# Exchanging row maxima and row sums between partition groups: copies in place of one-element reduces, and a later place for the row-sum reciprocal

## The chip, the cores and the metric

The kernel runs on one core of a Trainium2 chip. The metric is the device time of one execution in microseconds. TensorE (PE), VectorE (DVE), ScalarE (ACT) and GpSimd (POOL) run side by side, each in its own program order, and wait for each other by semaphores.

## The reference, cut to what matters

```python
# attention: batch 8, heads 8, seq 576, head_dim 64, float32
scores = scale * q @ k.T
thresh = max(scores, -1) - tau
attn   = exp(where(scores >= thresh, scores, -1e9) - max(scores))
attn   = attn / (sum(attn, -1) + 1e-9)
x      = attn @ v                       # to 4608 x 512
# feed-forward, d_ff 1536
out    = (silu(x @ w_gate) * (x @ w_val)) @ w_out
```

## The kernel before

From the second batch on (28 of 32 head pairs, 140 score tiles) the kernel works on "halved" tiles. The 128 partitions are four groups of 32. Two neighbouring groups hold the same 32 query rows, one against the first half of the keys, the other against the second. A row's maximum and its sum are therefore in two partition groups, and each group must fetch the other's value. That is the function meet:

```python
def meet(x, m):                                  # x: [128, m, 2 or 3]; m = 4, or 2 for the last tile of a pair
    for g in range(NG):                          # four groups
        o = g ^ 1                                # the neighbour
        nc.vector.tensor_reduce(out=x[g*G:(g+1)*G, 0:m, 1], in_=x[o*G:(o+1)*G, 0:m, 0:1],
                                axis=AX.X, op=ALU.max)      # a reduce over one element: a copy

def scores(seg, t):                              # a generator; halved case, cut
    # TensorE: scores into the PSUM tiles pss (two, or one for the last tile of a pair); there are two in all
    for x, tile_ in enumerate(pss):
        nc.vector.tensor_reduce(out=mx[:, 2*x:2*x+2, 0], in_=tile_[:, :, 0:SH], ..., op=ALU.max, negate=True)
    meet(mx, m)
    nc.vector.tensor_reduce(out=nm[:, 0:m], in_=mx[:, 0:m, :], axis=AX.X, op=ALU.min)
    nc.scalar.activation(th[:, 0:m], nm[:, 0:m], AF.Identity, bias=cut, scale=-1.0)
    for x in range(m):
        nc.scalar.activation(ps[x], scs[x], AF.Exp, bias=nm[:, x:x+1])
    yield
    turn(1)                                      # VectorE transposes an earlier tile
    for x in range(m):                           # threshold and row sum; frees the score PSUM
        nc.vector.scalar_tensor_tensor(out=ps[x], in0=scs[x], scalar=th[:, x:x+1], in1=ps[x],
                                       op0=ALU.is_ge, op1=ALU.mult, accum_out=sm[:, x, 0:1])
    meet(sm, m)
    nc.vector.tensor_reduce(out=tot[:, 0:m], in_=sm[:, 0:m, :], axis=AX.X, op=ALU.add)
    nc.vector.reciprocal(out=ri[:, 0:m], in_=tot[:, 0:m])
    yield
    for x in range(m):                           # scaling, on GpSimd
        nc.gpsimd.tensor_scalar(out=ps[x], in0=ps[x], scalar1=ri[:, x:x+1], scalar2=None, op0=ALU.mult)
    yield

# main loop, per tile, cut: the feed-forward products of earlier batches fill TensorE's time
go = scores(seg, t); next(go)
next(go); fill(part); next(go); fill(part)
```

## Time and profile before

| | before |
|---|---|
| median of 6 runs | 1625.6 us (1624.4 to 1627.6) |
| TensorE busy | 95% of the span |
| VectorE busy | 67% |
| GpSimd busy | 48%; 480 us of it are the 486 scalings of L319 |
| both exchanges on VectorE | 1120 reduces of about 0.15 us |

The prediction below shows most of the lines.

### The profile page before, as it was taken

Reading aid. Unit: us, or ns where it says so; the run is one execution under the profiler, and the core shown is the slowest. Engines: PE = TensorE matmul, PEld = TensorE weight load, DVE = VectorE, ACT = ScalarE, POOL = GpSimd, SP = SyncE. Lnnn points to the kernel's source line nnn. Section 1 sums busy time; section 2 is a strip of 40 time slices with the busy share of each in tenths; the row PEclk is TensorE's granted clock in tenths of the full one; section 3 lists DMA queues with packets and bytes.
Section 4 is the critical chain, followed back from the end, with each engine's and each line's share of the span. In section 5 each row is a group of like instructions: output and inputs, shape, how many; then the busy total and the mean of one; then the engine's idle time right before and its main releaser. Section 6 shows DMA issues by size and latency. Waiting matters only on the chain.

```text
span 1625.3 us, 29972 instructions
## 1 busy us (share of the span) xinstructions
PE 1548.6 (95%) x11344; PEld 1033.4 (64%) x11344; DVE 1081.0 (67%) x3618; ACT 604.1 (37%) x1304; POOL 780.6 (48%) x726
## 2 busy tenths in 40 slices
PE   6898779889999999999999999999999999999998
PEld 4675555347675776657666766675755675677865
DVE  6887888787777777767767777776776787500000
ACT  6776644223333333333333333343434343311110
POOL 3554455555555555545555455554655554511111
PEclk9899889999999999999999999999999999999999
DMA  7541221111111111011111111101111110000000
GB/s 171 144 138 59 69 50 30 43 43 31 37 37 37 37 37 31 18 32 37 30 43 37 37 37 30 39 13 36 31 43 37 37 31 28 1 14 7 7 13 13
DMA packets 176415, 66.82 MB, mean 41 GB/s; under 512 B 159632, under 2 KB 159632, under 8 KB 176272
## 3 DMA queue, kind: packets, MB, share of 16 engines
q1 hardware_dynamic: 173328, 55.47, 15.1%
q0 software_dynamic: 2944, 9.44, 1.7%
q8 instruction: 90, 1.47, 0.4%
q14 instruction: 53, 0.43, 0.1%
HBM read 55.44 MB, written 9.44 MB: 40 GB/s over the span
## 4 chain that ended last, share of the span: by engine, by line
PE 78%; DVE 9%; POOL 1%; ACT 1%; issue 1%; POOLq 0%; DVEq 0%; ACTq 0%
PE po L488 21%; PE pg L442 21%; PE pv L442 20%; PE sc L267 8%; PE xa L400 8%; DVE p L307 2%; DVE mx L287 2%; DVE p L333 1%; POOL p L319 1%; DVE mx L244 1%; ACT p L303 1%; DVE sums L244 0%; DVE wo L185 0%; ACT L303 0%; POOL ht L473 0%
## 5 line engine op out<-in xcount | busy, mean ns | idle before, releaser
L319 POOL TENSOR_SCALAR p<-p,ri 128x288 f32<-128x288 f32 x486 | 480.3, 1004 | 504.4 <-DVE ri L315 504.3
L442 PE MATMUL pg<-xall,wgv 128*128 128x256 f32 (+1 forms) x1824 | 403.0, 374 | 5.7 <-POOL wgv L190 5.7
L442 PE MATMUL pv<-xall,wgv 128*128 128x256 f32 (+1 forms) x1824 | 399.9, 373 | 0.0
L442 PEld LDWEIGHTS pg<-xall,wgv 128*128 128x128 f32 x1824 | 331.4, 192 | 75.7 <-issue 19.2
L442 PEld LDWEIGHTS pv<-xall,wgv 128*128 128x128 f32 x1824 | 331.0, 191 | 60.4 <-issue 11.6
L488 PE MATMUL po<-wo,ht 128*128 128x512 f32 x816 | 364.2, 598 | 4.6 <-POOL ht L473 4.6
L307 DVE SCALAR_TENSOR_TENSOR p<-sc,th,p 128x288 f32<-128x288 f32 (+1 forms) x540 | 258.7, 529 | 57.2 <-ACT p L303 56.1
L488 PEld LDWEIGHTS po<-wo,ht 128*128 128x128 f32 x816 | 151.1, 190 | 196.1 <-issue 186.2
L299 ACT ACTIVATE th<-nm,cut 128x4 f32<-128x4 f32 (+1 forms) x140 | 41.6, 297 | 539.7 <-DVE nm L290 539.7
L303 ACT ACTIVATE p<-sc,nm 128x288 f32<-128x288 f32 (+1 forms) x540 | 237.2, 512 | 0.7
L287 DVE TENSOR_REDUCE mx<-sc 128x2 f32<-128x576 f32 x252 | 179.5, 749 | 77.7 <-PE sc L267 77.6
L267 PE MATMUL sc<-kT,qT 64*32 64x288 f32 x4032 | 170.9, 415 | 29.4 <-DVE p L307 29.3
L462 DVE TENSOR_TENSOR ht<-gt,pv 128x512 f32<-128x512 f32 (+1 forms) x108 | 69.8, 646 | 191.6 <-PE pv L442 186.3
L333 DVE STREAM_TRANSPOSE p<-p 128x576 f32<-128x576 f32 x252 | 181.4, 754 | 4.3 <-POOL p L319 4.3
L473 POOL TENSOR_TENSOR ht<-ht,gt 128x512 f32<-128x512 f32 (+1 forms) x108 | 127.9, 1211 | 80.1 <-ACT gt L471 80.1
L267 PEld LDWEIGHTS sc<-kT,qT 64*32 64x32 f32 x4032 | 66.5, 106 | 121.8 <-issue 96.6
L400 PE MATMUL xa<-p,vall 64*64 64x288 f32 x2016 | 131.8, 412 | 9.8 <-issue 7.4
L456 ACT COPY gt<-pg 128x512 f32<-128x512 f32 (+1 forms) x114 | 65.0, 570 | 156.6 <-PE pg L442 156.6
L400 PEld LDWEIGHTS xa<-p,vall 64*64 64x64 f32 x2016 | 80.4, 135 | 60.9 <-issue 16.8
L244 DVE TENSOR_REDUCE sums<-sums 32x4 f32<-32x4 f32 (+1 forms) x560 | 83.9, 150 | 10.5
L411 DVE COPY xall<-xa 128x128 f32<-128x128 f32 x56 | 13.7, 286 | 115.2 <-PE xa L400 115.2
L244 DVE TENSOR_REDUCE mx<-mx 32x4 f32<-32x4 f32 (+1 forms) x560 | 83.1, 148 | 10.4
(78 smaller groups left out, 969.5 us busy)
## 6 DMA issues: line engine op xcount, KB each, us to landing
vall<-in_v_dram SPq DMA_DIRECT2D x112, 144.0 KB, 3.2
qraw<-in_q_dram SPq DMA_DIRECT2D x128, 72.0 KB, 2.4
kraw<-in_k_dram SPq DMA_DIRECT2D x128, 72.0 KB, 2.7
out_dram<-ob POOLq DMA_DIRECT2D x32, 256.0 KB, 2.4
wo<-in_moe_w_gate_dram SPq DMA_DIRECT2D x16, 384.0 KB, 3.5
wo<-in_moe_w_val_dram SPq DMA_DIRECT2D x16, 384.0 KB, 4.0
xall<-in_moe_w_out_dram SPq DMA_DIRECT2D x6, 768.0 KB, 5.3
wo<-in_moe_w_out_dram SPq DMA_DIRECT2D x2, 768.0 KB, 4.3
```

The source lines that it names most:

```text
L244: nc.vector.tensor_reduce(out=x[g * G:(g + 1) * G, 0:m, 1], in_=x[o * G:(o + 1) * G, 0:m, 0:1], axis=AX.X, op=ALU.max)
L267: nc.tensor.matmul(ps[g * G:(g + 1) * G, u, 0:SH], qT[hs, col + a * G:col + (a + 1) * G], kT[hs, c * SH:(c + 1) * SH], start=True, stop=True)
L287: nc.vector.tensor_reduce(out=mx[:, 2 * x:2 * x + 2, 0], in_=tile_[:, :, 0:SH], axis=AX.X, op=ALU.max, negate=True)
L303: nc.scalar.activation(ps[x], scs[x], AF.Exp, bias=nm[:, x:x + 1])
L307: nc.vector.scalar_tensor_tensor(out=ps[x], in0=scs[x], scalar=th[:, x:x + 1], in1=ps[x], op0=ALU.is_ge, op1=ALU.mult, accum_out=sm[:, x, ...
L319: nc.gpsimd.tensor_scalar(out=ps[x], in0=ps[x], scalar1=ri[:, x:x + 1], scalar2=None, op0=ALU.mult)
L333: nc.vector.transpose(out=p, in_=p)
L400: nc.tensor.matmul(xa[a][h * D:(h + 1) * D, at:at + n * G].rearrange("d (i q) -> d i q", q=G), vr[rs, h, j, :], p[rs, lo:lo + n, j, :], st ...
L442: nc.tensor.matmul(ps[:, i], wgv[:, mat, c, (f + i) * P:(f + i + 1) * P], x[:, c, cs], start=(c == 0), stop=(c == NCC - 1))
L462: nc.vector.tensor_tensor(out=hts[f // 2][:, :, 0:n], in0=gts[f // per][:, f % per:f % per + GR, :], in1=ps, op=ALU.mult)
L473: nc.gpsimd.tensor_tensor(out=ht, in0=ht, in1=gt[:, 2 * x:2 * x + 2, :], op=ALU.mult)
L488: nc.tensor.matmul(po, hts[f // 2][:, f % 2, i * P:(i + 1) * P], wo[:, f, :], start=(f == 0), stop=(f == NF - 1))
```

## The change

The intent, as it reads: take the exchange of sums off VectorE, give it to ScalarE, and compute sum and reciprocal later in VectorE's order, so that ScalarE's answer has time to come. With it, meet takes the copying function as an argument, and the maxima are now exchanged by VectorE's tensor_copy in place of the one-element tensor_reduce.

```diff
-    def meet(x, m):
+    def meet(x, m, copy):
         for g in range(NG):
             o = g ^ 1
-            nc.vector.tensor_reduce(out=x[g * G:(g + 1) * G, 0:m, 1], in_=x[o * G:(o + 1) * G, 0:m, 0:1],
-                                    axis=AX.X, op=ALU.max)
+            copy(x[g * G:(g + 1) * G, 0:m, 1:2], x[o * G:(o + 1) * G, 0:m, 0:1])
...
-            meet(mx, m)
+            meet(mx, m, nc.vector.tensor_copy)
...
-            meet(sm, m)
+            meet(sm, m, nc.scalar.copy)
+            yield
             nc.vector.tensor_reduce(out=tot[:, 0:m], ...)
...
         nc.vector.reciprocal(out=ri[:, 0:m], in_=tot[:, 0:m])
-        yield
+        if not halved:
+            yield
```

## The prediction

> **What bounds the kernel now.** I read the page's busy table first, then the windows by stage, then who waited for whom, then the timeline of single tiles. From the page:
>
> ```profile
> PE 1548.6 (95%) x11344; PEld 1033.4 (64%) x11344; DVE 1081.0 (67%) x3618; ACT 604.1 (37%) x1304; POOL 780.6 (48%) x726
> L319 POOL TENSOR_SCALAR p<-p,ri 128x288 f32<-128x288 f32 x486 | 480.3, 1004 | 504.4 <-DVE ri L315 504.3
> L244 DVE TENSOR_REDUCE sums<-sums 32x4 f32<-32x4 f32 (+1 forms) x560 | 83.9, 150 | 10.5
> L244 DVE TENSOR_REDUCE mx<-mx 32x4 f32<-32x4 f32 (+1 forms) x560 | 83.1, 148 | 10.4
> ```
>
> TensorE is the busiest engine. The two L244 groups are the exchanges that the change touches: 140 halved score tiles x 4 partition groups, for the row maxima (mx) and the row sums (sums). By stage (before the halved tiles; their first part, with the weights still being put together; the long part; the tail with feed-forward work alone):
>
> ```profile
> 0.00:166.00 166.00, 139.62 (x962) 96.93 (x963) 126.81 (x267) 115.72 (x211) 76.14 (x49) 0.94 0.46 126
> 166.00:345.00 179.00, 145.90 (x1148) 86.42 (x1146) 151.16 (x508) 73.27 (x164) 99.32 (x85) 0.90 0.22 52
> 345.00:1405.00 1060.00, 1052.44 (x8409) 700.99 (x8401) 784.26 (x2806) 385.09 (x874) 569.83 (x559) 1.00 0.15 33
> 1405.00:1625.30 220.30, 210.66 (x838) 149.09 (x836) 18.74 (x39) 30.05 (x55) 35.29 (x35) 0.99 0.03 10
> ```
>
> The columns are the stretch, its length, busy us of PE, PEld, DVE, ACT, POOL, then clock and DMA. From 345 to 1405 us PE is idle for only 7.6 us of 1060: nothing taken off another engine can gain more than that there. From 166 to 345 it is idle for 33 us, with DVE 84% busy. What PE waits for:
>
> ```profile
> PE sc L267 <- DVE p L307: 29.3, 22, 4.5
> PE xa L400 <- issue: 7.4, 1, 7.4
> ```
>
> So the only loop around PE that the change touches is: scores (sc) on PE, maximum of scores on DVE (L287), exchange of maxima (L244), nm (L290), exp on ACT, threshold and row sum on DVE (L307), which frees the two score buffers in PSUM for the next scores. One tile of it, with PE's load rows left out:
>
> ```profile
> 769.12 1.20 PE L267 MATMUL sc<-kT,qT 64*32 64x288 f32 x32
> ...
> 769.78 0.18 DVE L315 RECIPROCAL ri<-tot 128x4 f32<-128x4 f32 x1
> ...
> 770.05 3.95 POOL L319 TENSOR_SCALAR p<-p,ri 128x288 f32<-128x288 f32 x4 [6.47 <-DVE ri L315]
> ...
> 770.45 1.42 DVE L287 TENSOR_REDUCE mx<-sc 128x2 f32<-128x576 f32 x2
> 771.90 0.64 DVE L244 TENSOR_REDUCE mx<-mx 32x4 f32<-32x4 f32 x4
> 772.57 0.16 DVE L290 TENSOR_REDUCE nm<-mx 128x4 f32<-128x8 f32 x1
> ```
>
> The reader is to see that the exchange of maxima (771.90) begins while GpSimd is in its four scalings of the previous tile (770.05 to 774.00), and now is not held up by them: four reduces in 0.64 us, the usual.
>
> **What the Trainium skill says.** "SBUF — State Buffer", § Who interferes with whom: VectorE and GpSimd share one pair of SBUF ports under an exclusive lock; a VectorE copy in a 2-port mode takes it and waits for a GpSimd instruction in progress, while tensor_reduce never does on this chip. "VectorE: DVE Perf Modes", § What auto-detection actually checks: a one-source copy with both ends in SBUF and an even outer dimension goes into the 2-port mode by itself. The new exchange of maxima is a tensor_copy of 32x4 or 32x2 float32 in SBUF, so it qualifies. The trace of before has the same conflict with other instructions, two-port tensor_scalars of the weight work:
>
> ```profile
> 224.47 1.80 POOL L190 TENSOR_TENSOR wo<-wo,spare 128x768 f32<-128x768 f32 x1
> ...
> 224.57 2.25 DVE L181 TENSOR_SCALAR wo<-wo 128x768 f32<-128x768 f32 x1
> ```
>
> That L181 form takes 0.66 us in the median. Begun 0.1 us after a GpSimd instruction it took 2.25, to 0.5 us after GpSimd ended. The lock is real here; what no run has yet is how it treats four tiny copies against a train of four GpSimd instructions. "VectorE: DVE Perf Modes", § The TRN2 errata: a small SBUF operation costs mostly a fixed time per instruction; the trace agrees (142 to 156 ns for 2 or 4 elements), so a copy is hardly cheaper than the reduce it replaces. Same page, § Two Vector instructions with no wait between them: an instruction whose operands start in another quadrant than those before starts only after these have finished. Each of the four copies changes quadrant, so I expect them one after the other with a gap in which GpSimd can take the lock back.
>
> **The change part by part.**
> (1) Exchange of sums moves to ACT. DVE loses 560 x 0.150 = 84 us, ACT gains 560 copies; ACT's smallest copy now, 64x32, takes 180 ns, so about 100 us: ACT goes from 604 to some 705 us, 43% of the span. ACT has no part in the lock. The copies sit in ACT's order after the exps and before the evacuation of the next gate product, and wait for the last L307; that holds an evacuation by up to 1 us, which the four product buffers in PSUM should cover: 0 on PE. For DVE the saving counts only where DVE is the limit: the seven or so tiles between 166 and 230 us with weight pieces on DVE, 7 x 0.64 = 4.5 us. Elsewhere the work lay beside PE's scores (in the tile above DVE is done with ht before mx begins): 0.
> (2) tot and reciprocal come after the first half of the fill. In the instruction order of the changed kernel, 95 of the 140 tiles have nothing between L307 and tot: there DVE waits for the ACT copies, about 0.1 + 4 x 0.18 = 0.8 us in place of 0.64 on its own, so ri is 0.1 to 0.2 us later. In 40 tiles a product with the value branch (0.66 us) comes first, and in 5 weight work. GpSimd's scalings so start 0.2 to 1 us later, nearer to the next exchange of maxima. Their consumer, DVE's transposition, comes over a tile later (scaled 801.1 to 805.1, transposed 815.5), so this alone costs nothing.
> (3) Exchange of maxima becomes 560 DVE copies: without the lock, 0 to 10 ns each, nothing. With the lock: I followed GpSimd's work through the timeline at each of the 139 exchanges that have a later score tile. 99 begin while GpSimd is busy; its unbroken work then lasts another 1.88 us in the mean (186 us in all), but the single instruction in progress only 0.61 us (60 us in all). If the four copies have to take turns with the four scalings, the exchange is stretched by the first number, else by the second.
> How much reaches PE I took from each next score tile's slack: how long L307 had been done when PE got to it. In 345 to 1405, 29 of 118 tiles have under 0.3 us of it, 40 have 0.3 to 1.7 (mostly 1.5, a tile with one gate and one value product), 49 more; in 166 to 345, 17 of 21 have none. Stretch minus 0.1 us minus slack, where positive, sums to 20.7 + 62.9 = 84 us if turns are taken, and 6.2 + 10.6 = 17 us if not. Moving the scalings of the tiles with a value product between makes the first 99 us and leaves the second as it is.
> Sum: 1625 - 4.5 + 1 (the later ri) + something from 17 to 99. I don't hold the turn-taking for sure on every copy (in one place of the trace a GpSimd tensor_scalar let a VectorE instruction in halfway), so I take about 40: 1662 us.
>
> **The rivals.**
> A, no conflict at all: the copies are so short that they slip in. Then only (1) and (2) count: 1615 to 1626. Against it: every L181 that began under a GpSimd instruction was longer than its median.
> B, one wait per exchange: once the first copy has the lock, the other three follow before GpSimd's next. GpSimd's scalings follow each other at 0.985 us with records of 1.004, so its next is always ready. 1630 to 1645.
> C, turns for every copy: 1690 to 1725.
> D, the ACT round trip hurts: DVE waits for ACT in 95 tiles, and ACT may be late where it has sigmoids, table loads (1.28 us) or weight pieces ahead. 1625 to 1640, with no long copies. For it: the idle time before tot would appear. Against it: DVE waits for PE's scores just after anyway, 77.7 us at L287.
> I give A 0.15, B and D together 0.30, something between B and C 0.35, C 0.20.
>
> **Range and chances.** Slower by over 2% begins at 1657.8 us: all of C and most of between, 0.20 + 0.30 = 0.50, and a little of the others, 0.52. Faster by over 2% needs 32 us of PE idle time given back, nearly all of that in 166 to 345: 0.02. The rest 0.46. The range that should hold it 8 times in 10 leaves out the best part of A and the worst of C: 1622 to 1708.
>
> **What would show it.** Right: L244 copies of mx with a mean well over 0.15 us and single ones near 1 us, all where a POOL L319 runs; PE sc waiting for DVE p L307 grown from 29.3 us by the added time; 345 to 1405 with PE idle time; ACT near 705 us; sums copies of about 0.18 us on ACT; tot with idle time before it that ACT ended. Wrong: mx copies of 0.14 us beside L319, then the lock does not matter for such small copies and the time stays at 1615 to 1626; or a longer time with short copies, then it is D or PE waiting for an evacuation on ACT.

## More of the kernel before

One more view, part 4 of the page, is the chain that ended last, followed back from the end of the program; its shares tell which engine the end hung on:

```profile
PE 78%; DVE 9%; POOL 1%; ACT 1%; issue 1%; POOLq 0%; DVEq 0%; ACTq 0%
```

The end hangs mostly on TensorE, so a change on another engine shows up only if it makes TensorE wait longer or shorter.

## The result, and the profile after

The changed kernel takes 1701.5 us (median of 6 runs, 1697.3 to 1706.2). The ratio to the kernel before is 1.0467, with a 95% interval of 1.0446 to 1.0488: 76 us slower. Ratios here are the mean time of one kernel's fast runs over that of the other's fast runs of the same rounds, so not quite the ratio of the medians quoted; "so many us" below means the ratio minus one, times the 1626 us of before.

From the page after (lines of the kernel are moved by one or so; L319 of before is L320, L307 is L306):

```profile
PE 1585.5 (93%) x11344; PEld 1048.8 (62%) x11344; DVE 1103.2 (65%) x3058; ACT 716.3 (42%) x1864; POOL 779.6 (46%) x726
...
PE 66%; DVE 17%; ACT 5%; issue 2%; POOL 2%; DMA 0%; SPq 0%; DVEq 0%; POOLq 0%; ACTq 0%
...
L244 DVE COPY mx<-mx 32x4 f32<-32x4 f32 (+1 forms) x560 | 189.8, 339 | 10.5
...
L244 ACT COPY sums<-sums 32x4 f32<-32x4 f32 (+1 forms) x560 | 108.5, 194 | 165.5 <-DVE p L306 158.7
...
L312 DVE TENSOR_REDUCE tot<-sums 128x4 f32<-128x12 f32 (+1 forms) x140 | 23.0, 164 | 97.0 <-ACT sums L244 97.0
```

Three things stand out. VectorE executes 560 instructions fewer and is still busy 22 us longer. The exchange of maxima went from 83.1 to 189.8 us, 339 ns a copy in place of 148. And tot, which had nothing to wait for, now has 97 us of idle time before it, ended by ScalarE's copies. The chain of the end hangs on VectorE for 17% in place of 9%. What TensorE waits for, after:

```profile
PE sc L266 <- DVE p L306: 68.8, 49, 5.2
PE po L489 <- POOL ht L474: 9.1, 3, 4.0
```

The wait of the scores for L306, which frees the score buffers, went from 29.3 us in 22 waits to 68.8 us in 49. This counts only waits that the profile shows as idle time. PE's busy time grew as well, by 37 us (1548.6 to 1585.5). Of these, 18.5 us lie on the score matmuls (170.9 to 189.4), where a wait in the middle of a group, and the slower clock told of next, may be counted as busy. The other half lies on matmuls that don't wait for VectorE's score work. It goes with a slower TensorE: the mean granted clock (1 is full speed) was 0.981 to 0.987 in the runs of before and 0.969 to 0.974 in all six of the changed kernel. In stretches at half clock a gate or value matmul took 634 ns, elsewhere 379 (medians of both traces). From 345 us on, TensorE was never busy at half clock in the profile of before, and for 36 us in this one. By an estimate from these figures (36 us times 1 - 379/634) that costs about 15 us. No run holds the clock apart, so whether the waits bring it down is not shown.

The single copies are uneven: 156 ns at the least, 172 in the middle, 1703 at the most:

```profile
L244 DVE COPY mx<-mx x560: 156/172/1703, 167.5 to 1480.4; 32x4 f32<-32x4 f32 x150, 32x2 f32<-32x2 f32 x37
```

Where they are long, GpSimd is at work: the longest of the 143 copies that meet no tensor instruction of GpSimd in this trace took 0.31 us. From the timeline of the changed kernel, VectorE and GpSimd in one stretch (start, duration, instruction):

```profile
828.44 1.42 DVE L286 TENSOR_REDUCE mx<-sc 128x2 f32<-128x576 f32 x2 [1.69 <-PE sc L266]
828.79 3.72 POOL L474 TENSOR_TENSOR ht<-ht,gt 128x512 f32<-128x512 f32 x3
829.24 0.56 ACT L457 COPY gt<-pg 128x512 f32<-128x512 f32 x1
829.89 3.36 DVE L244 COPY mx<-mx 32x4 f32<-32x4 f32 x4
```

Four copies of four elements took 3.36 us in place of 0.64. The first three ended with GpSimd's three products (at 830.08, 831.30 and 832.54; the products at 830.06, 831.28 and 832.51), and the fourth took 0.70 us beside the query scaling that followed. Looked at one by one in narrower stretches of the same time, one copy and the product it had to sit out are:

```profile
830.02 1.26 POOL L474 TENSOR_TENSOR ht<-ht,gt 128x512 f32<-128x512 f32 x1
830.10 1.21 DVE L244 COPY mx<-mx 32x4 f32<-32x4 f32 x1
```

The copy begins 0.08 us after the product, ends 0.02 us after it, and the next copy (831.32) sits out the next product in the same way. Beside the scalings it is milder:

```profile
814.33 1.00 POOL L320 TENSOR_SCALAR p<-p,ri 128x288 f32<-128x288 f32 x1
814.39 0.46 DVE L244 COPY mx<-mx 32x4 f32<-32x4 f32 x1
```

Here the copy was done at 814.85, halfway through the scaling, which itself took no longer than usual. No copy that met scalings of L320 alone took over 1.01 us; the 27 copies of over 1.1 us met products, query scalings or weight work.

### The profile page after: what moved, and what is told of

Its sections match the earlier page's. It is cut to its first block, busy times and chain, and to the rows that moved or that the text cites. A ratio compares the mean times of both kernels' runs of the same rounds, so it can differ in the third digit from the quotient of the medians.

```text
span 1702.9 us, 30134 instructions
## 1 busy us (share of the span) xinstructions
PE 1585.5 (93%) x11344; PEld 1048.8 (62%) x11344; DVE 1103.2 (65%) x3058; ACT 716.3 (42%) x1864; POOL 779.6 (46%) x726
## 4 chain that ended last, share of the span: by engine, by line
PE 66%; DVE 17%; ACT 5%; issue 2%; POOL 2%; DMA 0%; SPq 0%; DVEq 0%; POOLq 0%; ACTq 0%
PE pg L443 17%; PE po L489 17%; PE pv L443 17%; PE sc L266 8%; PE xa L401 7%; DVE mx L244 5%; DVE p L306 4%; DVE mx L286 3%; DVE p L334 2%; ACT L302 1%; ACT p L302 1%; POOL p L320 1%; ACT sums L244 1%; DVE nm L289 0%; DVE wo L185 0%
## 5 line engine op out<-in xcount | busy, mean ns | idle before, releaser
L320 POOL TENSOR_SCALAR p<-p,ri 128x288 f32<-128x288 f32 x486 | 479.2, 1001 | 545.5 <-DVE ri L315 483.1
L443 PE MATMUL pv<-xall,wgv 128*128 128x256 f32 (+1 forms) x1824 | 405.7, 376 | 0.0
L489 PE MATMUL po<-wo,ht 128*128 128x512 f32 x816 | 370.8, 607 | 9.1 <-POOL ht L474 9.1
L443 PEld LDWEIGHTS pv<-xall,wgv 128*128 128x128 f32 x1824 | 335.1, 194 | 63.1 <-issue 14.0
L306 DVE SCALAR_TENSOR_TENSOR p<-sc,th,p 128x288 f32<-128x288 f32 (+1 forms) x540 | 258.6, 530 | 57.5 <-ACT p L302 56.6
L266 PE MATMUL sc<-kT,qT 64*32 64x288 f32 x4032 | 189.4, 427 | 69.4 <-DVE p L306 68.8
L244 DVE COPY mx<-mx 32x4 f32<-32x4 f32 (+1 forms) x560 | 189.8, 339 | 10.5
L266 PEld LDWEIGHTS sc<-kT,qT 64*32 64x32 f32 x4032 | 71.7, 108 | 173.2 <-issue 144.8
L244 ACT COPY sums<-sums 32x4 f32<-32x4 f32 (+1 forms) x560 | 108.5, 194 | 165.5 <-DVE p L306 158.7
L312 DVE TENSOR_REDUCE tot<-sums 128x4 f32<-128x12 f32 (+1 forms) x140 | 23.0, 164 | 97.0 <-ACT sums L244 97.0
```

What stands on the lines that cost most here:

```text
L244: copy(x[g * G:(g + 1) * G, 0:m, 1:2], x[o * G:(o + 1) * G, 0:m, 0:1])
L266: nc.tensor.matmul(ps[g * G:(g + 1) * G, u, 0:SH], qT[hs, col + a * G:col + (a + 1) * G], kT[hs, c * SH:(c + 1) * SH], start=True, stop=True)
L443: nc.tensor.matmul(ps[:, i], wgv[:, mat, c, (f + i) * P:(f + i + 1) * P], x[:, c, cs], start=(c == 0), stop=(c == NCC - 1))
L489: nc.tensor.matmul(po, hts[f // 2][:, f % 2, i * P:(i + 1) * P], wo[:, f, :], start=(f == 0), stop=(f == NF - 1))
```

## The experiments

Two theories were open: the VectorE copies of the maxima held up by GpSimd ("the lock"), and the round trip over ScalarE with the later reciprocal. Twelve kernels ran; all gave right results.

### Taking the two parts of the change apart

**e1_max_reduce.** The changed kernel, with the maxima by reduce again:

```diff
-            meet(mx, m, nc.vector.tensor_copy)
+            meet(mx, m, reduce_copy)      # the one-element tensor_reduce
```

> The changed kernel, with the maxima exchanged by tensor_reduce again; sums on ScalarE and the later sum and reciprocal stay. If VectorE's copies of the maxima, held up by GpSimd, cost the time: 1616 to 1632 us, PE sc waiting for L306 about 25 to 35 us as before. If the ScalarE round trip and the later reciprocal cost a good part of it: 1650 to 1685 us, with the waits of tot for ACT (97 us in the changed kernel) still there. If the two only hurt together: near 1625 here and near 1625 in the next run too.

Measured: 1634.1 us, ratio 1.0044 (1.0027 to 1.0060): +7 us, 2 us above the range for held-up copies. TensorE's wait for L306's counterpart and tot's wait for ScalarE:

```profile
PE sc L269 <- DVE p L309: 32.9, 27, 3.7
...
DVE tot L315 <- ACT sums L244: 97.0, 130, 1.4
```

Most of the loss is gone, though ScalarE's copies and the wait for them are all there.

**e2_max_copy_only.** The kernel before, with only the maxima by copy:

```diff
-            meet(mx, m)                   # reduces
+            meet(mx, m, nc.vector.tensor_copy)
```

> The kernel before, with the maxima exchanged by VectorE copies and nothing else changed. Held-up copies as the cause: 1675 to 1705 us, copies of mx near 0.34 us in the mean as in the changed kernel. ScalarE round trip as the cause: 1625 to 1645 us. A part each: 1650 to 1675.

Measured: 1690.7 us, ratio 1.0394 (1.0378 to 1.0409): +64 us, nothing moved to ScalarE. Its exchange lines:

```profile
L244 DVE COPY mx<-mx 32x4 f32<-32x4 f32 x448 | 150.4, 336 | 8.4
L247 DVE TENSOR_REDUCE sums<-sums 32x4 f32<-32x4 f32 x448 | 67.3, 150 | 8.4
L244 DVE COPY mx<-mx 32x2 f32<-32x2 f32 x112 | 35.4, 316 | 2.1
```

The copies take 185.8 us against the 83.1 of the reduces. So one call in the diff, which the change's intent does not speak of, carries 64 of the 76 us. With e1's 7 that makes 71; the 5 left lie at the edge of the intervals.

**e3_early_sum.** The changed kernel, with tot and reciprocal right after ScalarE's copies:

```diff
             meet(sm, m, nc.scalar.copy)
-            yield
             nc.vector.tensor_reduce(out=tot[:, 0:m], ...)
```

> The changed kernel with tot and reciprocal emitted right after the exchange of sums, so that VectorE waits for ScalarE in all 140 tiles. If the late place matters by moving GpSimd's scalings into the exchange of maxima: faster than the changed kernel by 10 to 20 us, 1680 to 1692. If the place matters little: 1695 to 1710.

Measured: 1709.2 us, ratio 1.0506 (1.0490 to 1.0523). It is slower than the changed kernel, not faster, by about 6 us; the guess that the late place drives GpSimd into the exchange at a net cost fell. Given ScalarE's copies, the late place is the better one.

**e4_sum_copy_only.** The kernel before, with the sums by VectorE copies and the maxima by reduces:

```diff
-            meet(sm, m)                   # reduces
+            meet(sm, m, nc.vector.tensor_copy)
```

> The kernel before, with the sums exchanged by VectorE copies and the maxima by reduces. The same 560 copies as in the second run, at another place of the tile, where GpSimd's scalings of the tile before are mostly done. Lock theory: few copies held up, mean under 0.2 us, 1622 to 1640 us. If a copy between quadrants is slow in itself, wherever it stands: as much as the second run.

Measured: 1626.0 us, ratio 0.9999 (0.9984 to 1.0014). Its copies:

```profile
L244 DVE COPY sums<-sums 32x4 f32<-32x4 f32 x448 | 75.4, 168 | 8.5
```

The same 560 copies on the same engine cost nothing here: at this place of the tile the scalings are mostly over, and a copy takes 168 ns. In the trace 131 of the 140 exchanges of sums meet no GpSimd work; the few that do are held up here too, up to 1.36 us for one copy. So it is not the copy that is slow but the copy beside GpSimd.

### Is it the lock?

**f3_max_copy_to_psum.** The changed kernel whole, but the copies of the maxima write to unused columns of the score tile in PSUM:

```diff
-            meet(mx, m, nc.vector.tensor_copy)
-            nc.vector.tensor_reduce(out=nm[:, 0:m], in_=mx[:, 0:m, :], axis=AX.X, op=ALU.min)
+            other = pss[0][:, 0, SH + 32:SH + 32 + m]
+            for g in range(NG):
+                o = g ^ 1
+                nc.vector.tensor_copy(other[g * G:(g + 1) * G], mx[o * G:(o + 1) * G, 0:m, 0])
+            nc.vector.tensor_tensor(out=nm[:, 0:m], in0=mx[:, 0:m, 0], in1=other, op=ALU.min)
```

> The changed kernel whole, but the VectorE copies of the maxima write to unused columns of the score tile in PSUM, and the minimum of own and other maxima is a tensor_tensor. Same count of copies at the same place, with one end in PSUM, where the two-port mode needs both in SBUF. Lock theory: no copy over 0.3 us although GpSimd runs beside them, time 1630 to 1640 as with reduces. If a small copy between quadrants is slow beside any GpSimd work, or by its place in the tile: 1690 to 1705.

Measured: 1638.2 us (1634.5 to 1643.3), ratio 1.0072 (1.0047 to 1.0097); the interval overlaps that of e1. All its copies (shortest, middle, longest):

```profile
L291 DVE COPY sc<-mx x560: 150/162/169, 164.8 to 1410.0; 32x4 f32<-32x4 f32 x150, 32x2 f32<-32x2 f32 x37
```

Same operation, same count, same place, GpSimd as busy as ever (780 us; 118 of the 140 exchanges begin while it works): with one end outside SBUF the longest of 560 copies took 169 ns, against 1703. This is the behaviour that the lock of the two-port mode asks for, and a slow copy between partition groups does not.

**f4a_act_scaling** is a base: the kernel before, with the scalings on ScalarE in place of GpSimd (the diff shows this edit). **f4b_act_scaling_max_copy** is the same with the maxima by VectorE copies:

```diff
-            if halved and not split:      # scaling on GpSimd
+            if False:                     # always on ScalarE
```

> The kernel before with the 486 scalings of the probabilities on ScalarE in place of GpSimd, as a base for the next run; both exchanges by reduce. ScalarE gets about 280 us more and stays under 60% of the span: 1625 to 1660.

> The run before this one, with the maxima exchanged by VectorE copies. If GpSimd's work beside the copies is the cause, and the scalings the larger part of it: copies of mx under 0.25 us in the mean (0.336 with the scalings on GpSimd), and only 10 to 40 us above the run before this one, from the output products and the query scaling that stay on GpSimd. If GpSimd's scalings have little to do with it: 55 us or more above it.

Measured: f4a 1634.1 us, ratio 1.0053 (1.0038 to 1.0068); f4b 1672.2 us, ratio 1.0292 (1.0274 to 1.0309). The copies cost 38 us here (1.0292 / 1.0053, times 1626), where they cost 64 with the scalings on GpSimd.

```profile
L244 DVE COPY mx<-mx 32x4 f32<-32x4 f32 x448 | 105.1, 235 | 8.4
L244 DVE COPY mx<-mx 32x2 f32<-32x2 f32 x112 | 20.5, 183 | 2.1
```

In f4b's timeline, 117 of the 140 exchanges meet no GpSimd work and take 0.68 us in the mean. The other 23 meet output products, query scalings or weight work and are stretched by 37 us together. So a few long hold-ups cost almost what they last, and taking the scalings away removes 26 of the 64 us. I had expected the scalings to be the larger part; they are the more frequent one but not the costlier one.

### The rest: ScalarE's round trip and the late place

**f1_late_only** is the kernel before with only the late place of tot and reciprocal, both exchanges by reduce. **f2_act_sums_early** is the kernel before with only the sums on ScalarE, tot and reciprocal right after.

```diff
 # f1
             meet(sm, m)
+            yield
 # f2
-            meet(sm, m)
+            for g in range(NG):
+                o = g ^ 1
+                nc.scalar.copy(sm[g * G:(g + 1) * G, 0:m, 1:2], sm[o * G:(o + 1) * G, 0:m, 0:1])
```

> The kernel before with one change: sum and reciprocal of the rows come after the first half of the fill; both exchanges stay reduces on VectorE. Of the 8 us that ScalarE exchange plus late place cost (1634 against 1626): if the late place makes GpSimd late for the output products, 1630 to 1636; if the ScalarE copies are what costs, 1624 to 1628.

> The kernel before with one change: the sums exchanged by ScalarE copies, sum and reciprocal right after them, so that VectorE waits for ScalarE in every tile. If the ScalarE round trip costs: 1634 to 1645, more than with the late place, as the changed kernel was 8 us better than its early form. If the late place is what costs: 1624 to 1629.

Measured: f1 1631.4 us, ratio 1.0019 (1.0002 to 1.0036), +3 us. The median lies in the range for a late GpSimd, one of the four runs (1627.1) in the other, and TensorE's wait for the output products grew only from 4.6 to 5.8 us, so that reason is not shown. f2 1641.4 us, ratio 1.0089 (1.0074 to 1.0105), +14 us. In f2's waits of VectorE:

```profile
DVE tot L314 <- ACT sums L313: 129.0, 140, 2.2
```

VectorE has 83 us less work than before (998 against 1081 us busy), and the kernel is slower: it stands still for 0.92 us per tile in place of working for 0.64. An in-order engine that waits at the head of its queue is as occupied as one that works. With the late place +14 comes down to e1's +7, and tot's wait for ScalarE from 129.0 to 97.0 us.

### How much of a longer exchange reaches TensorE

**f5_max_reduce_twice** and **f8_max_reduce_thrice**: the kernel before with the exchange of maxima done two and three times, by reduces that the lock does not touch. This is a known dose, the same in each tile.

```diff
             meet(mx, m)
+            meet(mx, m)                   # f5; once more for f8
```

> The kernel before with the exchange of maxima done twice by reduces: the same stretch of 0.64 us in every tile, 90 us in all, where the held-up copies stretched it by 107 us in all, unevenly. Static slack count of the timeline of before: 28 us reach TensorE, 1650 to 1658. If the count itself is too low because a late tile makes the next late: 1665 to 1685; then the unevenness of the stretch has little part in the 64 us.

> The kernel before with the exchange of maxima done three times by reduces, 1.28 us longer in every tile, 179 us in all. A count of slack tile by tile gives 63 us (28 for the exchange done twice, where 46 were measured). A count in which a tile's lateness is carried into the next wherever VectorE does not wait for TensorE's scores gives 48 for twice and 120 for thrice. So carried lateness: 1735 to 1755 us. One tile at a time: 1685 to 1700.

Measured: f5 1672.0 us, ratio 1.0278 (1.0263 to 1.0294), +45 us; f8 1728.9 us, ratio 1.0640 (1.0622 to 1.0658), +104 us. TensorE's wait for the score buffers, f5 and then f8:

```profile
PE sc L267 <- DVE p L308: 47.7, 45, 3.8
```

```profile
PE sc L267 <- DVE p L309: 84.3, 83, 4.5
```

The prediction's way of counting took each tile alone: stretch minus the slack until TensorE comes for the buffers. It gives 28 and 63 us, both too low. The second way, made after f5's result, carries lateness on: VectorE's lateness at an exchange is TensorE's own, or what was left from the tile before less the idle time that VectorE had before its mx reduce, whichever is larger, plus the stretch of this tile; what of it exceeds the slack becomes TensorE's lateness. In the timeline of before VectorE waits for TensorE's scores in 96 of the mx reduces only, so often nothing absorbs it. This gives 48 and 120 us against the 45 and 104 measured: near for the first, 16 too high for the second (which is below the range I gave). A recount from the trace gives 26 and 60 for one tile at a time, 47 and 118 for carried lateness, so the counts themselves are good to some 3 us. Fed with the stretches that e2's trace shows, start of the first copy to end of the fourth, less 0.64 us (102 us in all), the carried count gives 65 us, the one-tile count 47; e2 measured 64.

That the carried count meets e2's 64 so closely is in part luck, because neither count knows of the clock. From 345 us on TensorE was busy at half clock for 29 us in e2's profile, 13 in f5's, 20 in f8's and 0 in that of before. By the estimate above that is about 12, 5 and 8 us. As far as these counts go, most of what the one-tile count lacks for f8 (41 us) is then lateness handed on; for e2 the clock could be most of the 17 us lacking. How these 17 divide stays open.

### A try at something better

**f7_sum_next_tile.** As e1, but tot and reciprocal only after the next tile's nm, when ScalarE's copies are long done:

```diff
+        finish()                          # after the exps: tot, reciprocal and scaling of the tile before
         yield
...
-            next(go)                      # tot, reciprocal, scaling after the first half of the fill
+            unfinished.append(go)         # in the next tile
```

> A try at a version that beats both: maxima exchanged by reduces, sums by ScalarE copies, and sum and reciprocal only after the next tile's nm, when ScalarE's copies are long done, so that VectorE waits for nothing. VectorE is freed of 90 us without a new wait. If VectorE's time at any place of the tile reaches TensorE at about half: 1600 to 1618. If only time on the way from scores to the freed score buffers counts: 1622 to 1632, as 0.35 us moves into that way in place of 1.1 us that lay beside TensorE's scores.

Measured: 1629.8 us, ratio 1.0027 (1.0012 to 1.0042), 4 us slower than before. The waits of its VectorE:

```profile
DVE mx L289 <- PE sc L269: 139.1, 101, 5.8
```

Of tot's wait for ScalarE 0.9 us is left, VectorE works 99 us less than before, and what came of it is more waiting: mx waits for TensorE's scores 139.1 us in place of 77.6, and the products with the value branch (ht) wait for ScalarE's copies 56.2 us in place of 1.1. TensorE's wait for the score buffers stayed at 30.1 us. Taking VectorE's work away beside TensorE's scores gained nothing; the kernel before remains the best of all that ran (e4 equals it).

## Why the prediction was right or wrong

It forecast +36 us and got +76; direction and mechanism held, the size did not.

- **The bound and the loop: right.** TensorE was the limit, and the time came in where TensorE waits for L306 to free the score buffers.
- **The exchange of maxima as the costly part, by the lock: right, and shown.** e2 has 64 of the 76 us with this edit alone. f3 removes it with the copies kept, and e4 has the same copies where GpSimd is done. In e2's trace all 31 copies of over 0.25 us that began under a product (ht) ended within 0.03 us of its end. The sign "all where a POOL L319 runs" was too narrow: the longest copies are not those beside scalings. The evidence from L181 was also weaker than it sounds: of the eight that began under GpSimd's work three were only 0.01 us over the median.
- **Term (3), "something from 17 to 99 … I take about 40": this is the term that failed.** It measured 64 (e2). Two things went into it. The stretch was offered as 186 us with turns and 60 with one wait (recounted: 207 and 62); it was 103 us of copy time (185.8 less 83.1), because products make the copies take turns and scalings let them in halfway. That lay inside what was offered. The step that failed is the share of it that reaches TensorE, taken off tile by tile as though each tile began anew: with e2's true stretches this count gives 47 us of the 64. f5 and f8 show the same error with no lock in it, 45 and 104 us measured against 28 and 63. Lateness carried from tile to tile can account for most of what is lacking in f8, but the carried count is too high there (120), and in e2 the lower clock could account for about 12 of the 17 us lacking. So that the share was too small is shown, and how it divides between the two is not.
- **The time lies in the range of rival C, and that is luck.** C was turns for every copy and a stretch of 186 us or more, of which 84 to 99 reach TensorE. What ran had about half the stretch, and a larger share of it reached TensorE.
- **Terms (1) and (2), "-4.5" and "+1": their sum is wrong in sign.** They are +7 together (e1) in place of -3.5. I held the wait of tot for ScalarE to be harmless because VectorE waits for TensorE's scores just after. f2 shows +14 for it when nothing hides it. The 4.5 us hoped for between 166 and 230 us did not appear as a gain of the whole time in any of e1, f2 and f7.
- **Rival D** was put at no more than 15 us and with no long copies; it is real at 7, and came on top of the copies, not in their place. **Rival A** is excluded by the copies' lengths. Between **B** and **C** the truth depends on GpSimd's instruction.
- **The late place bringing GpSimd nearer to the exchange:** counted at 84 to 99 us if turns are taken. The copies of the changed kernel last 4 us longer in all than e2's (189.8 against 185.8), and the sum of e1 and e2 falls 5 us short of the change; but e3, with the early place, is slower still. Whether those 5 us are this effect stays open.
- **ScalarE's busy time:** 705 us expected, 716 measured; a copy took 194 ns, not 180.

How the pieces of the miss add up: 1625 + 64 + 7 + 5 = 1701.

## What to carry to other kernels

Before replacing one small VectorE instruction by another of the same length, ask which SBUF ports it takes and what GpSimd does at that moment: here a one-element reduce served as a copy that GpSimd did not hold up. To size a delay on an in-order engine that is not the bottleneck, don't take the slack off tile by tile; lateness can be handed on wherever that engine does not come to rest, and a known dose (the same harmless instruction once more) measures the share in one run. Look at the granted clock too before giving the whole of a difference to waits. Work moved to another engine frees nothing if its result is waited for at the head of the queue, and freed time is worth something only on the path that the bottleneck waits for.

## What the Trainium skill lacked or had wrong

- "SBUF — State Buffer", § Who interferes with whom, says that whichever side starts first holds the shared pair for the whole instruction. For GpSimd's tensor_tensor of 128x512 the runs agree (a copy begun 0.08 us into a product of 1.26 us ended 0.02 us after it). For GpSimd's tensor_scalar of 128x288 they don't: a copy begun 0.06 us into a scaling of 1.00 us was done 0.52 us into it. In e2's trace, of 191 copies of over 0.2 us beside scalings 84 ended at the middle of one, and 100 where one gives way to the next. The 69 exchanges that met scalings alone took 1.22 us in the mean and 1.51 at most, where four waits for whole scalings would be near 4 us.
- The same section says that tensor_reduce never contends on this chip. The runs agree: the 560 one-element reduces of the maxima in the kernel before, 108 of whose 140 exchanges met GpSimd's work, stayed between 142 and 154 ns. No page says that such a reduce therefore serves as a copy that stays off the lock.
- "VectorE: DVE Perf Modes", § Why PSUM operands drop a tier, says that a PSUM operand rules out the two-port mode. f3 agrees and shows a use that the page does not draw: 560 copies with one end in PSUM stayed between 150 and 169 ns beside GpSimd, as against up to 1703 ns within SBUF.
- "VectorE: DVE Perf Modes", § The TRN2 errata, gives 58 cycles plus the elements (fewer in a faster mode) for a VectorE instruction within SBUF, by an estimate from the page's clock at most 65 ns for four elements, and says itself that its fixed term is rather 150 cycles. The runs side with the second: 156 ns at the least for such a copy.
